# Stack loads spread over 44 steps, the second matrix block loaded apart, and a unit's steps moved, in a kernel of attention and Fourier mixing

## The chip, the cores and the metric

The kernel runs on one core of a Trainium2 chip. The metric is the device time of one execution in microseconds; three runs of the kernel before stand behind its median. One further execution was taken by the hardware profiler, and all rows of a trace come from it. The engines are called PE (matmul), PEld (its weight loads), DVE (vector), ACT (scalar), POOL (GpSimd) and SP (sync, which here only issues DMAs). Each works through its own instructions in order and waits for the others by semaphores. DMAs are issued by SP and by POOL.

## The reference

The input is one sequence of 2048 rows with 640 columns. Two results are computed from it, 32-head attention with heads of 20 columns and the real part of a two-dimensional Fourier transform, and a sigmoid gate of each row mixes them.

```python
def reference(A_x, A_wqkv, A_wo, B_x, B_dft_seq_re, B_dft_seq_im, B_dft_hid_re, B_dft_hid_im, gate_w):
    # _A_ref: attention, 32 heads of 20
        scores = jnp.einsum("bhqd,bhkd->bhqk", q, k) * (Dh ** -0.5)
        p = _softmax(scores, axis=-1)
        o = jnp.einsum("bhqk,bhkd->bhqd", p, v)
    # _B_ref: transform along the columns, then along the rows, real part
        a = jnp.einsum("bsd,ed->bse", x, dft_hid_re)
        b = jnp.einsum("bsd,ed->bse", x, dft_hid_im)
        y = jnp.einsum("ts,bse->bte", dft_seq_re, a) - jnp.einsum("ts,bse->bte", dft_seq_im, b)
    ...
    x = A_x
    g = _sigmoid((x * gate_w).sum(-1, keepdims=True))
    return g * a + (1 - g) * b
```

## The kernel before, in words

**Units and steps.** The main loop walks through 32 units. A unit is a pair of heads and half of the queries (1024 of them); two units make a pair of heads. A unit has 32 steps, so there are 1024 steps; a step scores 128 keys against 512 queries for both heads. Scores are computed twice. The first time (L159) gives the maxima: VectorE reduces each block of 512 (L161). The second time (L682) takes two more rows, in which the maximum is subtracted inside the matmul, and ACT takes the exponential (L684). The maxima run 41 steps ahead of the exponentials. Every four steps make a cycle whose order of scores (`e`, `m`) and fill work (`F`) is written out in `ORDER`; at its end (`B`) the averages over the values follow (L445).

**The fill work** that stands between the scores is the Fourier half: first the transform along the columns (L298), then, from step 228, the one along the rows (L520), 16 DFT steps to a tile of output, with a saving of products in which matrices and halves are first added (`PRODUCTS`). One matrix block of 128 x 1024 serves eight DFT steps. `load_c` loads it in one or two parts of 512 KB on SP's queue (L410); its `finish` adds the two parts on POOL (L416) and splits the sum into a leading and a trailing part (L102, L103), which the matmuls read as `part`. A block is loaded at DFT step 0 of eight, three blocks ahead, and finished at DFT step 4, two blocks ahead. The first part goes to a tile `raw` of three buffers, the second to `raw2` of two. In the same way `load_a` loads the other operand (L425) and POOL prepares it (L430, L102, L103). At the end of a tile POOL adds the result to what stands in memory (L551).

**Stacks.** `load_stack` brings the keys (`kst`) and queries (`qst`) of the next pair from memory in twelve DMAs on POOL's queue (L632): four for the keys, four for the queries of the pair's first unit, four for those of its second. They are emitted at steps 2, 4, ... 24 of the pair that runs. The maxima of the next pair begin in that pair's step 23, those of its second unit in step 55. Pair 9, say, is loaded in units 15 and 16, counted as the units whose results leave then.

**The end of a unit.** `unit_end` copies the averages to `o` and hands seven pieces of work to later steps (L485): the row sums go to memory (L459) and come back in another shape (L462), DVE takes their reciprocal (L465), this goes to memory (L468) and comes back spread over partitions as `rb` (L472), POOL multiplies (L475), and `o` is stored (L483). All of these DMAs are on SP's queue.

**The rows of the maxima.** When a unit's maxima are done, `max_chain` transposes them and splits them on DVE, and two steps later SP writes four rows into `qst` (L198, L199). This happens in step 26 of a unit, and the exponentials of the unit that needs them begin in step 32, that is, with the next unit.

**The order** within an engine is the order of emission. `at_step` puts work off to the beginning of a later step, in the order in which it was handed over.

Of the kernel before, what the change touches and what calls it, by code (L numbers as in the profile page):

```python
# [10 lines left out]
F32 = mybir.dt.float32  # L11
# [7 lines left out]
P = 128  # L19
# [10 lines left out]
NU = 2 * NP  # L30
# [15 lines left out]
PRODUCTS = (  # L46
# [7 lines left out]
)  # L54
HT = NS // 2
UNITS = len(PRODUCTS) * HT


def f32(ap):
    return ap.bitcast(F32)  # L60
# [3 lines left out]
def mix_kernel(ctx: ExitStack, tc: tile.TileContext, xa, wqk, wb, cdft, wo, out):  # L64
    nc = tc.nc
    pe, act, dve, pool, sp = nc.tensor, nc.scalar, nc.vector, nc.gpsimd, nc.sync
# [48 lines left out]
    def pair_tile():  # L115
        return work.tile([P, 2, 512], F32, name="p", bufs=5)

    def raw_tile():
        return work.tile([P, 1024], F32, name="raw", bufs=3)

    def part_tile():
        return work.tile([P, 2, 1024], R, name="part", bufs=3)
# [4 lines left out]
    def load_stack(p):  # L127
        kt, qt = kst[p % 2], qst[p % 2]
        u = S // 2
        for t, o, two, one, cs in ((kt, D, 0, 2, slice(0, S)), (qt, 0, 1, 0, slice(0, u)), (qt, 0, 1, 0, slice(u, S))):  # L130
            for h in range(2):
                r = (2 * p + h) * DH
                b = 64 * h
                rows = slice(o + r, o + r + DH)
                yield f32(t[b + two * DH : b + (two + 2) * DH, cs]), qk_scr[:, rows, cs]
                yield f32(t[b + one * DH : b + (one + 1) * DH, cs]), qk_scr[0, rows, cs]
# [8 lines left out]
    def at_step(i, fn):  # L145
        later.setdefault(i, []).append(fn)
# [254 lines left out]
    cfin, rest = [], []  # L401

    def load_c(g):
        n, j = divmod(g, 2)
        n, t = divmod(n, HT)
        raws = []
        for i, (_, th, ri) in enumerate(PRODUCTS[n][0]):
            raw = apool[0].tile([P, 1024], F32, name="raw2", bufs=2) if i and apool else raw_tile()
            o = (2 * ri + j) * 1024
            sp.dma_start(raw, cdft[th * HT + t, :, o : o + 1024])  # L410
            raws.append(raw)

        def finish():
            c = cparts[g] = part_tile()
            if len(raws) > 1:
                pool.tensor_tensor(raws[0], raws[0], raws[1], op=ALU.add if PRODUCTS[n][0][1][0] > 0 else ALU.subtract)  # L416
            split(c[:, 0], c[:, 1], raws[0], pool, pool)

        return finish

    def load_a(n, s):
        raws = []
# [27 lines left out]
    def unit_end(i, n):  # L450
        o = pa.tile([P, 512], F32, name="o")
        act.activation(o, av, AF.Copy)
        lc = pa.tile([P, 16], F32, name="lc")
        rb = pa.tile([P, 512], F32, name="rb")

        q = pool if n == NU - 1 else sp

        def store_l():
            q.dma_start(l_scr[n], o.rearrange("(j r) c -> j r c", j=4)[:, DH])  # L459

        def load_l():
            q.dma_start(lc, l_scr[n].rearrange("j (a b) -> (j a) b", b=16))  # L462

        def recip():
            dve.reciprocal(lc, lc)  # L465

        def store_r():
            q.dma_start(r_scr[n].rearrange("j (a b) -> (j a) b", b=16), lc)  # L468

        def load_r():  # L470
            for j in range(4):
                q.dma_start(rb[32 * j : 32 * j + 32, :], r_scr[n, j : j + 1].to_broadcast([32, 512]))  # L472

        def norm():
            pool.tensor_tensor(o, o, rb, op=ALU.mult)  # L475

        def store_o():
            for qc in range(2):
                for h in range(2):
                    j = 2 * qc + h  # L480
                    t0 = (n % 2) * (S // 2) + qc * 512
                    r = (2 * (n // 2) + h) * DH
                    q.dma_start(o_scr[r : r + DH, t0 : t0 + 512], o[32 * j : 32 * j + DH, :])  # L483

        steps = (1, 4, 10, 12, 15, 23, 25) if n < NU - 2 else (1, 4, 10, 12, 15, 19, 21)  # L485
        for k, fn in zip(steps, (store_l, load_l, recip, store_r, load_r, norm, store_o)):
            if n == NU - 1:
                rest.append(fn)
            else:
                at_step(i + k, fn)  # L490
# [7 lines left out]
    def dft_step(g):  # L498
        n, t, s = g // NS // HT, g // NS % HT, g % NS
        if s == 0:  # L500
            new_y(0), new_y(1)
            outs[n, t] = []
            for _, th, hf in PRODUCTS[n][2]:
                tt = th * HT + t
                y = None
                if (tt, hf) in signs:
                    y = apool[0].tile([P, HE], F32, name="yt", bufs=4)
                    sp.dma_start(y, y_scr[tt, :, hf * HE : (hf + 1) * HE])
                outs[n, t].append(y)
        if s % 8 == 0 and g // 8 + 3 < 2 * UNITS:  # L510
            cfin.append(load_c(g // 8 + 3))
        if s % 8 == 4 and cfin and g // 8 + 2 < 2 * UNITS:
            cfin.pop(0)()
        c = cparts[g // 8]
        cs = slice((s % 8) * P, (s % 8 + 1) * P)
        a = at[n % 2, s]
        for z, (cz, az) in enumerate(((0, 0), (0, 1), (1, 0))):
            for h in range(2):
                r = slice(64 * h, 64 * h + 64)
                pe.matmul(yp[h][:, :HE], c[r, cz, cs], a[r, az], start=s == 0 and z == 0, stop=s == NS - 1 and z == 2)  # L520
            if z < 2:
                yield
        w = g % (HT * NS) - 16
        if n + 1 == len(PRODUCTS) and w >= 0:
            d, r = divmod(w, 8)
            if r == 0 and d < ND:
                wos[d] = raw_tile()[:, :D]
                sp.dma_start(wos[d], wo[:, d])
            if r == 5 and d < ND:
                raw = wos.pop(d)  # L530
                for h in range(2):
                    wos[d, h] = a_tile(1, 2 * d + h)
                    split(wos[d, h][:, 0], wos[d, h][:, 1], raw[:, h * HE : (h + 1) * HE], pool, pool)
        if s == NS - 1:
            m = apool[0].tile([P, HE], F32, name="m", bufs=2)
            y0, y1 = yp[0][:, :HE], yp[1][:, :HE]

            def read():
                act.activation(m, y0, AF.Copy)
                dve.tensor_tensor(m, y1, m, op=ALU.add)  # L540

            extras.append((now[0], read))
            for out_, y in zip(PRODUCTS[n][2], outs.pop((n, t))):
                extras.append((now[0] + 5, functools.partial(finish_y, out_, t, m, y)))
        yield
# [29 lines left out]
    apool = []  # L575
# [25 lines left out]
    HID = 4 * NS - HEAD  # L601
# [26 lines left out]
    def begin(i):  # L628
        now[0] = i
        n, s = divmod(i, 32)  # L630
        for fn in later.pop(i, ()):
            fn()  # L632
        if s % 2 == 0:
            flush()
        if s == 0 and n % 2 == 0:
            p = n // 2
            if p + 1 < NP:
                at_step(i + 6, functools.partial(load_v, p + 1))
                for j, args in enumerate(load_stack(p + 1)):
                    at_step(i + 2 + 2 * j, functools.partial(pool.dma_start, *args))  # L640
        if i < total:
            pts[n, s // 2, s % 2] = pair_tile()

    def end(i):
        if start + 2 <= i < start + 2 + HT:
            for k in range(2):
                at_step(i + 3, load_a(0, 2 * (i - start - 2) + k))
        if i % 4 == 2:
            c = i // 4
            if c + HEAD in (NS, 2 * NS):  # L650
                at_step(i + 2, load_wb(3 + (c + HEAD) // NS, pool, pool))
            if c in (HID - 5, HID - 3):
                at_step(i + 4, load_c((c - HID + 5) // 2))
            if c == HID + 1:
                cfin.append(load_c(2))
        if total - 10 <= i < total - 4 and i % 2 == 0:
            tt = (i - total + 10) // 2
            fins[tt] = load_o(tt)
        if i == total - 3:
            fins[0]()  # L660
# [71 lines left out]
    for tt in range(NS):  # L732
        y, o = ys.pop(tt), ops.pop(tt)
# [53 lines left out]
```

## Time and profile before

| | us |
|---|---|
| median of 3 runs | 1962.29 |
| lowest, highest | 1959.55, 1966.06 |
| the profiled execution | 1970.17 |
| its span, first to last instruction | 1968.4 |
| first start of the exponentials' scores, last | 270.8, 1889.2 |
| maxima on DVE (L161, 2048 of 683 ns) | 1287.9 |
| exponentials on ACT (L684, 2048 of 599 ns) | 1081.3 |
| POOL: sums and splits of matrix blocks (L416, L102, L103) | 187.8, 116.2, 267.0 |

A group's row gives the line, the engine, the operation, what it writes and reads, the count, then busy time and the mean of one in nanoseconds, then the engine's idle time just before these instructions and what ended it. A row of a timeline gives start and duration in microseconds, and in brackets the idle time before it and its releaser. The mean granted clock of TensorE was 0.990 of full speed over the span.

### The profile page before, as it was taken

To read this page: it belongs to the slowest core of one execution; us is meant where nothing else is said; L and a number is where in the kernel's file an instruction comes from. 1 tells how busy PE (TensorE), PEld (TensorE's weight loads), DVE (VectorE), ACT (ScalarE), POOL (GpSimd) and SP (SyncE) were. 2 spreads that over 40 slices of the span, in tenths; PEclk is the share of its full clock that TensorE was granted. 3 is DMA by queue.
4 is the path that set the end of the run, shared out by engine and by line. 5 is a ranking of instruction groups with operands and counts; after the bars stand their busy time and mean duration, and the time that the engine had idled before them with its cause. 6 is when DMAs were issued, how large, how long until landed. Compare 5 with 4: busy or idle time off the path is not lost. (4 is left out here: it accounts for less than half of the span.)

```text
span 1968.4 us, 43695 instructions
## 1 busy us (share of the span) xinstructions
PE 1932.7 (98%) x17080; PEld 1384.1 (70%) x17080; DVE 1455.3 (74%) x2419; ACT 1212.9 (62%) x2337; POOL 1045.3 (53%) x975
## 2 busy tenths in 40 slices
PE   8999999999999999999999999999999999999999
PEld 7987767777775666666666666666666666666679
DVE  4145568888897888887888878788888887888323
ACT  4221147777776676776676766666777766766741
POOL 1210001111005989556569967995786789687522
PEclk9999999999998999999999999999999999999999
DMA  7663321313124485435366746654554565554355
GB/s 222 172 170 126 131 97 46 81 57 81 38 62 144 160 227 149 122 114 142 99 174 198 195 152 183 211 170 121 145 176 124 179 171 173 158 153 148 97 158 183
DMA packets 196414, 281.02 MB, mean 143 GB/s; under 512 B 73272, under 2 KB 137816, under 8 KB 194288
## 3 DMA queue, kind: packets, MB, share of 16 engines
q1 hardware_dynamic: 158992, 246.20, 40.7%
q0 software_dynamic: 37216, 32.03, 6.7%
q8 instruction: 134, 2.20, 0.5%
q14 instruction: 72, 0.59, 0.1%
HBM read 213.81 MB, written 63.70 MB: 141 GB/s over the span
## 5 line engine op out<-in xcount | busy, mean ns | idle before, releaser
L161 DVE TENSOR_REDUCE mx<-ps 128x1 f32<-128x512 f32 x2048 | 1287.9, 683 | 203.6 <-PE ps L159 176.6
L684 ACT ACTIVATE p<-ps 128x512 f32<-128x512 f32 x2048 | 1081.3, 599 | 457.4 <-PE ps L159 254.3
L159 PE MATMUL ps<-kst,qst 60*128 60x512 f32 x2048 | 777.8, 427 | 9.8 <-DVE mx L161 3.8
L682 PE MATMUL ps<-qst,kst 62*128 62x512 f32 x2048 | 705.3, 424 | 7.8 <-DMA qst<-m 6.2
L520 PE MATMUL yp<-a,part 64*128 64x320 f32 x5376 | 687.5, 309 | 0.1
L520 PEld LDWEIGHTS yp<-a,part 64*128 64x128 f32 x5376 | 594.3, 186 | 15.5 <-DVE m L540 0.3
L445 PE MATMUL av<-p,v 128*21 128x512 f32 x4096 | 500.1, 605 | 0.1
L682 PEld LDWEIGHTS ps<-qst,kst 62*128 62x128 f32 x2048 | 339.0, 185 | 220.4 <-DVE mx L161 179.3
L159 PEld LDWEIGHTS ps<-kst,qst 60*128 60x128 f32 x2048 | 365.5, 185 | 39.5 <-DVE mx L161 12.5
L103 POOL TENSOR_TENSOR part<-raw,part 128x1024 fp32r<-128x1024 f32 x112 | 267.0, 2384 | 9.0
L445 PEld LDWEIGHTS av<-p,v 128*21 128x21 f32 x4096 | 98.8, 101 | 228.8 <-issue 225.2
L298 PE MATMUL yp<-wb,xs 64*128 64x320 f32 x1920 | 239.8, 312 | 3.1 <-ACT raw L306 3.0
L298 PEld LDWEIGHTS yp<-wb,xs 64*128 64x128 f32 x1920 | 209.7, 189 | 8.3 <-ACT raw L306 3.6
L416 POOL TENSOR_TENSOR raw<-raw,raw 128x1024 f32<-128x1024 f32 x78 | 187.8, 2407 | 17.5 <-DMA raw<-in_cdft 13.1
L102 POOL CAST part<-raw 128x1024 fp32r<-128x1024 f32 x112 | 116.2, 1037 | 124.6 <-PE yp L520 81.8
L102 POOL CAST wb<-raw 128x966 fp32r<-128x966 f32 (+1 forms) x4 | 3.4, 852 | 216.8 <-DMA raw<-in_wb 196.8
L551 POOL TENSOR_TENSOR yt<-yt,m 128x320 f32<-128x320 f32 x64 | 55.3, 873 | 114.2 <-DVE m L540 110.7
L475 POOL TENSOR_TENSOR o<-o,rb 128x512 f32<-128x512 f32 x32 | 41.3, 1292 | 130.9 <-DMA rb<-r_scr 71.1
L103 POOL TENSOR_TENSOR a<-araw,a 128x320 fp32r<-128x320 f32 x112 | 97.5, 871 | 9.0
L103 DVE TENSOR_TENSOR p<-ps,p 128x512 fp32r<-128x512 f32 x40 | 27.5, 691 | 94.8 <-ACT p L100 92.1
L106 PE MATMUL ps<-xs,part 128*128 128x512 f32 x200 | 80.6, 403 | 7.4 <-ACT xs L100 6.1
L100 ACT ACTIVATE p<-ps 128x512 fp32r<-128x512 f32 x40 | 23.8, 597 | 102.6 <-PE ps L108 102.6
(67 smaller groups left out, 1337.4 us busy)
## 6 DMA issues: line engine op xcount, KB each, us to landing
raw<-in_cdft SPq DMA_DIRECT2D x192, 512.0 KB
araw<-a_scr SPq DMA_DIRECT2D x192, 160.0 KB
qk_scr<-p SPq DMA_DIRECT2D x40, 512.0 KB
kst<-qk_scr POOLq DMA_DIRECT2D x32, 320.0 KB, 12.5
qst<-qk_scr POOLq DMA_DIRECT2D x64, 160.0 KB, 8.5
a_scr<-raw SPq DMA_DIRECT2D x64, 160.0 KB
yt<-y_scr SPq DMA_DIRECT2D x64, 160.0 KB
y_scr<-yt SPq DMA_DIRECT2D x64, 160.0 KB
```

The costliest lines, as they stand in the source:

```text
L102: e1.tensor_copy(dst1, src)
L103: e2.tensor_tensor(dst2, src, f32(dst1), op=ALU.subtract)
L106: pe.matmul(ps, st1, mv1, start=first, stop=False)
L159: pe.matmul(ps, q[b : b + KROWS, qt * P : (qt + 1) * P], k[b : b + KROWS, kc * 512 : (kc + 1) * 512], start=True, stop=True)
L161: return lambda: dve.tensor_reduce(mx[n][:, h, qt, kc : kc + 1], ps, axis=AX.X, op=ALU.max)
L298: pe.matmul(yp[h][:, :HE], xs[r, xz, d, cs], w[r, wz, d, :HE], start=d == 0 and z == 0, stop=d == ND - 1 and z == 2)
L416: pool.tensor_tensor(raws[0], raws[0], raws[1], op=ALU.add if PRODUCTS[n][0][1][0] > 0 else ALU.subtract)
L445: pe.matmul(av[32 * j : 32 * j + DH + 1, :], v[:, kt, h * (DH + 1) : (h + 1) * (DH + 1)], pp[qc][:, h, :], start=kt == 0, stop=kt == NS - 1)
L520: pe.matmul(yp[h][:, :HE], c[r, cz, cs], a[r, az], start=s == 0 and z == 0, stop=s == NS - 1 and z == 2)
L551: pool.tensor_tensor(y, y, m, op=ALU.add if sg == signs[tt, hf] else ALU.subtract)
L682: pe.matmul(pt, k[b : b + KROWS + 2, kt * P : (kt + 1) * P], q[b : b + KROWS + 2, qc * 512 : (qc + 1) * 512], start=True, stop=True)
L684: act.activation(pts[n, kt, qc][:, h], pt, AF.Exp, scale=float(DH) ** -0.5)
```

## The change

Three places are touched.

1. `load_c` returns two functions, `load` and `finish`. Each call of `load` issues one part. The first part is issued at DFT step 0 of eight as before, the second at DFT step 4, directly after the `finish` of the block before it. The first blocks, before the loop of DFT steps runs, still get both parts at once.
2. For all units but the last two, the steps of `unit_end` are 1, 5, 13, 15, 18, 24, 26 in place of 1, 4, 10, 12, 15, 23, 25.
3. The twelve stack DMAs are emitted at steps 2, 4, 6, 8, 11, 13, 15, 17, 32, 36, 40, 44 in place of 2 to 24. The last four are the queries of the second unit. Their order among themselves is the same.

```diff
-        for i, (_, th, ri) in enumerate(PRODUCTS[n][0]):
-            raw = apool[0].tile([P, 1024], F32, name="raw2", bufs=2) if i and apool else raw_tile()
-            o = (2 * ri + j) * 1024
-            sp.dma_start(raw, cdft[th * HT + t, :, o : o + 1024])
-            raws.append(raw)
+
+        def load():
+            i = len(raws)
+            if i < len(PRODUCTS[n][0]):
+                _, th, ri = PRODUCTS[n][0][i]
+                raws.append(apool[0].tile([P, 1024], F32, name="raw2", bufs=2) if i and apool else raw_tile())
+                o = (2 * ri + j) * 1024
+                sp.dma_start(raws[i], cdft[th * HT + t, :, o : o + 1024])
...
-        return finish
+        load()
+        return load, finish
...
-        steps = (1, 4, 10, 12, 15, 23, 25) if n < NU - 2 else (1, 4, 10, 12, 15, 19, 21)
+        steps = (1, 5, 13, 15, 18, 24, 26) if n < NU - 2 else (1, 4, 10, 12, 15, 19, 21)
...
-        if s % 8 == 4 and cfin and g // 8 + 2 < 2 * UNITS:
-            cfin.pop(0)()
+        if s % 8 == 4:
+            if cfin and g // 8 + 2 < 2 * UNITS:
+                cfin.pop(0)[1]()
+            if cfin:
+                cfin[0][0]()
...
-                for j, args in enumerate(load_stack(p + 1)):
-                    at_step(i + 2 + 2 * j, functools.partial(pool.dma_start, *args))
+                for j, args in zip((2, 4, 6, 8, 11, 13, 15, 17, 32, 36, 40, 44), load_stack(p + 1)):
+                    at_step(i + j, functools.partial(pool.dma_start, *args))
...
-                at_step(i + 4, load_c((c - HID + 5) // 2))
+                load, finish = load_c((c - HID + 5) // 2)
+                load()
+                at_step(i + 4, finish)
             if c == HID + 1:
                 cfin.append(load_c(2))
+                cfin[0][0]()
```

## The prediction

> **What bounds the kernel now.** First the page: span, engine times and the PE groups with their idle time.
>
> ```profile
> span 1968.4 us, 43695 instructions
> PE 1932.7 (98%) x17080; PEld 1384.1 (70%) x17080; DVE 1455.3 (74%) x2419; ACT 1212.9 (62%) x2337; POOL 1045.3 (53%) x975
> L159 PE MATMUL ps<-kst,qst 60*128 60x512 f32 x2048 | 777.8, 427 | 9.8 <-DVE mx L161 3.8
> L682 PE MATMUL ps<-qst,kst 62*128 62x512 f32 x2048 | 705.3, 424 | 7.8 <-DMA qst<-m 6.2
> ```
>
> PE is busy 98% of the span, and the change takes no matmul away. So it can only win or lose where PE stands still, and in the slow clock that follows. PE's own timeline has four such places in the main loop that lie beside moved work:
>
> ```profile
> 905.83 0.50 PE L159 MATMUL ps<-kst,qst 60*128 60x512 f32 x1 [2.12 <-DVE mx L161]
> 1142.68 0.83 PE L682 MATMUL ps<-qst,kst 62*128 62x512 f32 x2 [3.02 <-DMA qst<-m]
> 1247.37 0.59 PE L682 MATMUL ps<-qst,kst 62*128 62x512 f32 x2 [3.22 <-DMA qst<-m]
> 1638.32 0.76 PE L159 MATMUL ps<-kst,qst 60*128 60x512 f32 x1 [3.30 <-DMA qst<-qk_scr]
> ```
>
> What each costs is read from ten-microsecond windows: us, busy time of PE, PEld, DVE, ACT, POOL, then the granted clock and the DMA engines' share.
>
> ```profile
> 609.00:619.00 10.00, 7.01 (x47) 4.99 (x47) 4.08 (x8) 3.81 (x7) 7.37 (x6) 0.74 0.17 60
> 903.00:913.00 10.00, 7.88 (x62) 4.26 (x61) 5.78 (x11) 4.30 (x10) 7.44 (x9) 0.83 0.70 191
> 1139.00:1149.00 10.00, 6.97 (x49) 3.34 (x49) 4.07 (x7) 3.66 (x8) 9.35 (x6) 0.83 0.19 70
> 1244.00:1254.00 10.00, 6.78 (x49) 3.75 (x48) 4.63 (x9) 4.12 (x9) 9.65 (x10) 0.83 0.33 99
> 1634.00:1644.00 10.00, 6.70 (x41) 3.44 (x38) 4.00 (x8) 3.00 (x6) 9.70 (x9) 0.69 0.68 205
> 1010.00:1020.00 10.00, 10.00 (x100) 7.05 (x88) 7.63 (x14) 6.84 (x14) 5.37 (x6) 1.00 0.88 224
> ```
>
> The last row is an undisturbed stretch. A window's loss is its idle time plus (1 - clock) x 10 us: 2.1 + 1.7 = 3.8 us at 905; 3.0 + 1.7 = 4.7 at 1142; 3.2 + 1.7 = 4.9 at 1247; 3.3 + 3.1 = 6.4 at 1638. Together 19.8 us, the most that the change can win there. The window at 609 (a loss of 5.6 us) belongs to the change of stage, where the edits move little; it stays.
>
> A step is (1889.2 - 270.8) / 1024 = 1.58 us, from the first and last start here:
>
> ```profile
> L682 PE MATMUL ps<-qst,kst x2048: 386/397/792, 270.8 to 1889.2; 62*128 62x512 f32 x187
> ```
>
> The stalls lie at steps about 399 (unit 11's results, pair 7's load), 543 (unit 15, pair 9), 607 (unit 17, pair 10) and 855 (unit 25, pair 14): always a unit in which a stack is loaded.
>
> **The reciprocal.** At 905 PE waited for VectorE's maxima, and VectorE for this:
>
> ```profile
> 904.98 0.25 DVE L465 RECIPROCAL lc<-lc 128x16 f32<-128x16 f32 x1 [2.22 <-DMA lc<-l_scr]
> ```
> ```profile
> 892.81 0.32 SPq L462 DMA_DIRECT2D lc<-l_scr  x1
> ```
>
> The small load took 904.98 - 892.81 = 12.2 us. The change issues it one step later and the reciprocal three steps later: two steps (3.2 us) more distance against 2.22 us of waiting. Behind the reciprocal on VectorE stand the maxima, whose banks PE waits for, so the whole stall goes: **-3.8 us**. Bounds: -3.8, and 0 if the load, now behind one more issue of L425 on SP, lands over 3 us later than it did.
>
> **The normalization, and the rows behind it.** At 1142 and 1247 PE waited for the rows of the maxima (L198, L199). SP issues them behind the stores of `o` (L483), and those wait for POOL's L475:
>
> ```profile
> 1131.83 1.30 POOL L475 TENSOR_TENSOR o<-o,rb 128x512 f32<-128x512 f32 x1
> ...
> 1236.51 1.30 POOL L475 TENSOR_TENSOR o<-o,rb 128x512 f32<-128x512 f32 x1
> ```
> ```profile
> 1237.83 1.42 SPq L483 DMA_DIRECT2D o_scr<-o  x4
> 1239.30 1.72 SPq L410 DMA_DIRECT2D raw<-in_cdft  x2
> 1241.11 0.68 SPq L198 DMA_DIRECT2D qst<-m  x1
> ```
>
> L475 starts with no gap: POOL is behind its queue, and what counts is how much stands ahead. These are POOL's prices:
>
> ```profile
> L632 POOL DMA_DIRECT2D qst<-qk_scr x120 | 69.3, 585 | 25.2 <-DMA kst<-qk_scr 25.1
> L430 POOL TENSOR_TENSOR araw<-araw 128x320 f32<-128x320 f32 x80 | 69.9, 874 | 5.9 <-DMA araw<-a_scr 5.5
> L102 POOL CAST a<-araw 128x320 fp32r<-128x320 f32 x112 | 50.4, 450 | 21.4 <-DMA araw<-a_scr 16.2
> L103 POOL TENSOR_TENSOR a<-araw,a 128x320 fp32r<-128x320 f32 x112 | 97.5, 871 | 9.0
> L551 POOL TENSOR_TENSOR yt<-yt,m 128x320 f32<-128x320 f32 x64 | 55.3, 873 | 114.2 <-DVE m L540 110.7
> ```
>
> In these units three of the four issues for the second unit's queries (steps 18, 20, 22) stood ahead of L475 and now stand 14 steps or more behind it: 3 x 0.585 = 1.76 us earlier. L475 itself goes from step 23 to 24; nothing else in POOL's program changes place with it in units 15 and 17. (In units 9, 13 and 28 part or all of a matrix block's work slips ahead; none of them is among the late ones.) SP keeps its order: stores of `o`, now at step 26, then the rows of the same step. Further, one of the two L410 issues between L483 and the rows goes away, about half of the 1.72 us at 1239; I count 0.5 us at 1142 and 1.1 us at 1247. At 1142 the idle time falls from 3.0 to 3.0 - 1.76 - 0.5 = 0.8 us. Does a stall this short still lose the clock? The nearest rows:
>
> ```profile
> 262.93 0.50 PE L106 MATMUL ps<-xs,part 128*128 128x512 f32 x1 [1.31 <-ACT part L100]
> ```
> ```profile
> 260.00:270.00 10.00, 8.56 (x37) 6.40 (x36) 2.14 (x3) 1.82 (x3) 0.00 (x0) 1.00 0.34 130
> ```
>
> 1.31 us idle kept clock 1.00, 2.12 us at 905 lost it. So 0.8 is left of 4.7: **-3.9 us**. At 1247 the second matrix block takes back a part (next); its rows come about 1.76 + 1.1 - 0.8 = 2.1 us sooner, 1.1 us idle is left and with some chance of the clock I take 1.5: **-3.4 us**. Bounds for both: 0 (POOL finds another wait and is no sooner) and -9.6.
>
> [...]
>
> **The second matrix block** is loaded four DFT steps later in the program, but SP runs ahead of its emission, so often it moves by a few issues only. Around pair 10's load:
>
> ```profile
> 1201.43 0.86 SPq L410 DMA_DIRECT2D raw<-in_cdft  x2
> 1202.34 0.42 SPq L437 DMA_DIRECT2D v<-v_scr  x1
> 1207.61 0.85 SPq L425 DMA_DIRECT2D araw<-a_scr  x2
> ```
> ```profile
> 1215.43 2.43 POOL L416 TENSOR_TENSOR raw<-raw,raw 128x1024 f32<-128x1024 f32 x1 [4.26 <-PE av L445]
> ```
>
> In the changed order it comes directly behind the load of `v`: about 0.9 us later. POOL's wait before the sum at 1215 cannot be for PE's averages, which L416 does not read; I take it for the block's landing, and the price as **0.8 us** on POOL (used above). From 0.4 (an issue) to 4.3 (the wait doubles). Elsewhere POOL runs ahead of its need and a wait there is covered by its later waits (L551's 114.2 us above).
>
> **The first unit's queries** keep their place in POOL's program but for the last piece, which goes from step 16 to 17 and so behind one preparation of `a`: 0.874 + 0.450 + 0.871 = 2.2 us, in pair 9 also behind one L551 (3.1 us). Their landing and PE's first use:
>
> ```profile
> L632 POOL DMA_DIRECT2D qst<-qk_scr x1: 542/542/542, 1118.1 to 1118.1; - x1
> ...
> DMA to landing us min/median/max: 6.1/6.1/6.1
> ```
> ```profile
> L632 POOL DMA_DIRECT2D qst<-qk_scr x2: 519/576/634, 1221.4 to 1222.0; - x2
> ...
> DMA to landing us min/median/max: 7.7/7.9/8.2
> ```
> ```profile
> 1125.87 0.40 PE L159 MATMUL ps<-kst,qst 60*128 60x512 f32 x1
> ```
> ```profile
> 1230.32 0.40 PE L159 MATMUL ps<-kst,qst 60*128 60x512 f32 x1
> ```
>
> Pair 9 lands at 1124.2 with 1.7 us to spare, pair 10 at 1229.7 with 0.6 us, pair 14 is already late (1638). At full price: 3.1 - 1.7 = 1.4, 2.2 - 0.6 = 1.6, and 2.2 us more: 5.2 us. Transfers that leave these units may shorten the landing; I take half, **+2.6 us**. Bounds: -6.4 (the stall at 1638 goes) and 5.2 + 3 x 1.7 of clock = +10.3.
>
> **Other moves, at nothing.** `rb` has 6 steps from its issue to L475 in place of 8. Where POOL runs early it will wait there, and L475 still comes before step 24; if that cover went, POOL would lose up to two steps, 3.2 us, in such a unit. SP's wait for `r_scr` before L472 keeps its three steps, with the loads of `a` and of the matrix blocks queued behind it as now, only later in the unit. The second unit's queries, first needed at step 55, are issued by step 44: 11 steps, 17 us, for landings of 6 to 8 us in the rows above. POOL in those units carries the same four issues, 2.3 us, ahead of a later L475. Without this cover each pair would stall as at 1638, up to 6.4 us.
>
> **Sum.** -3.8 - 3.9 - 3.4 + 2.6 = -8.5 us. The profiled execution took 1970.17 us (span 1968.4); the median of the runs is 1962.29, and I carry the sum over unchanged: **1953.8, forecast 1954 us**, -0.43%.
>
> **Rivals.** *Slower: the last query piece decides.* If every one of the three is late at full price and loses the clock (+10.3), and POOL, waiting for matrix blocks that come late, brings L475 no sooner, then only the reciprocal is won: -3.8 + 10.3 = +6.5, 1968.8 us. It decides from 0.6 us of lateness in pair 10. For it: that margin, and DMA engines at 0.68 around 1638; against it: idle under 1.3 us kept the clock. 0.18. *Nothing to speak of: the wait is only handed on.* The reciprocal is won, L475 gains nothing, the pieces cost their 2.6: -1.2, 1961.1 us. For it: POOL's 4.26 us gap ahead of L475 at 1215, into which earlier work falls. 0.34. *All four stalls go*, the unloaded units' DMA relief reaching pair 14: -19.8, 1942.5 us. Against it: the piece at 1638 is issued later, not sooner. 0.10. *The change does not do what it says*: the second block is not apart in time, since SP runs ahead; true in the rows above, and without a time of its own.
>
> **How the numbers follow.** 0.38 for the forecast, 0.10, 0.34 and 0.18 for the others. A change under 0.3% (5.9 us) cannot be told from none here. Faster: 0.38 + 0.10 = 0.48; within: 0.34; slower: 0.18. The likeliest one's own range is 1951 (the query pieces cost nothing) to 1958 (one of the rows' terms is not won); the cases on both sides widen it to 1943 (all four stalls) and 1967 (most of the slower case).
>
> **What would show it.** Right: no gap before the reciprocal at step 397; L475 in units 15 and 17 some 1 to 2 us sooner by step and the rows' stalls under 1 us at full clock. The query term: PE waiting for `qst<-qk_scr` at steps 535, 599, 855. Wrong, if these gaps are gone and the time is not, if new waits for `part` or `raw` stand before PE, or if the stalls simply sit in other units.

## The result, and the profile after

The changed kernel is slower by 0.5%. Ratios are taken over runs on the same chips.

| | us |
|---|---|
| before, median of 6 runs beside it | 1960.68 (1958.47 to 1966.06) |
| changed, median of 6 runs | 1973.48 (1971.20 to 1974.39) |
| ratio | 1.0053, 95% interval 1.0039 to 1.0067 |
| profiled execution, before and changed | 1970.17, 1974.10 |
| forecast | 1954, range 1943 to 1967 |

The two profiled executions lie closer together than the medians: that of before, at 1970.17, is longer than each of its six runs. First the groups of PE and POOL in the changed kernel (L692 was L682, L419 was L416, L479 was L475, L639 was L632):

```profile
L159 PE MATMUL ps<-kst,qst 60*128 60x512 f32 x2048 | 778.3, 428 | 24.1 <-DMA qst<-qk_scr 15.0 <-issue 4.9 <-DVE mx L161 1.7
L692 PE MATMUL ps<-qst,kst 62*128 62x512 f32 x2048 | 703.5, 423 | 1.5 <-DVE mx L161 1.1 <-ACT p L694 0.3
...
L419 POOL TENSOR_TENSOR raw<-raw,raw 128x1024 f32<-128x1024 f32 x78 | 187.0, 2397 | 65.5 <-DMA raw<-in_cdft 52.5 <-PE ps L159 6.9 <-PE ps L692 5.5
...
L479 POOL TENSOR_TENSOR o<-o,rb 128x512 f32<-128x512 f32 x32 | 41.4, 1292 | 165.2 <-DMA rb<-r_scr 158.1 <-DMA out_y<-p 4.0 <-DMA yt<-y_scr 2.4
```

The wait for the rows of the maxima (6.2 us ahead of L682 before) is gone. The wait for the queries ahead of L159 has grown from 3.3 us to 15.0, and the 4.9 us put down to "issue" stands at the same kind of place, below. POOL's idle time ahead of the sums of matrix blocks has grown to 65.5 us. This is the group that answers to it in the kernel before:

```profile
L416 POOL TENSOR_TENSOR raw<-raw,raw 128x1024 f32<-128x1024 f32 x78 | 187.8, 2407 | 17.5 <-DMA raw<-in_cdft 13.1 <-PE av L445 4.3
```

PE's timeline of the changed kernel has four stalls of more than 2.2 us in the main loop, all before the first maxima of a new pair (pairs 5, 9, 10 and 14):

```profile
723.37 0.76 PE L159 MATMUL ps<-kst,qst 60*128 60x512 f32 x1 [4.58 <-DMA qst<-qk_scr]
...
1128.37 0.76 PE L159 MATMUL ps<-kst,qst 60*128 60x512 f32 x1 [4.85 <-issue]
...
1235.68 0.76 PE L159 MATMUL ps<-kst,qst 60*128 60x512 f32 x1 [5.33 <-DMA qst<-qk_scr]
...
1642.41 0.76 PE L159 MATMUL ps<-kst,qst 60*128 60x512 f32 x1 [5.12 <-DMA qst<-qk_scr]
```

The ten-microsecond windows around them, and two at the places of before's stalls behind the reciprocal and the rows:

```profile
719.00:729.00 10.00, 5.63 (x39) 3.34 (x41) 3.40 (x9) 1.96 (x5) 9.71 (x9) 0.83 0.62 192
1124.00:1134.00 10.00, 5.63 (x35) 3.22 (x35) 3.10 (x5) 1.82 (x4) 9.65 (x9) 0.66 0.48 167
1231.00:1241.00 10.00, 5.32 (x30) 2.67 (x30) 2.48 (x4) 1.32 (x3) 9.71 (x9) 0.70 0.76 217
1637.00:1647.00 10.00, 4.88 (x30) 2.70 (x31) 3.26 (x6) 2.26 (x5) 9.71 (x8) 0.71 0.67 211
903.00:913.00 10.00, 10.00 (x104) 7.87 (x100) 9.32 (x16) 7.66 (x15) 5.75 (x6) 1.00 0.57 162
1139.00:1149.00 10.00, 10.00 (x96) 6.71 (x90) 7.77 (x14) 7.18 (x15) 9.76 (x8) 1.00 0.39 110
```

By the prediction's own count (idle time and lost clock) the four lose 6.1, 7.8, 7.7 and 8.0 us, 29.6 together, against 6.4 us for late queries before. Where the reciprocal and the rows of unit 15 had cost 3.8 and 4.7 us, nothing is lost any more.

Why the queries are late is read at pair 10, from three views: SP's timeline before and after, then POOL's after. In the kernel before, SP issued both parts of the block that POOL sums at 1195.36 together:

```profile
1189.16 0.95 SPq L410 DMA_DIRECT2D raw<-in_cdft  x2
1197.33 0.55 SPq L459 DMA_DIRECT2D l_scr<-o  x1
```

After, the second part stands behind the store of the row sums (L463, before L459), and that waits until the unit ends:

```profile
1189.11 0.43 SPq L414 DMA_DIRECT2D raw<-in_cdft  x1
1197.16 0.54 SPq L463 DMA_DIRECT2D l_scr<-o  x1
1197.81 0.39 SPq L414 DMA_DIRECT2D raw<-in_cdft  x1
```
```profile
1193.41 1.80 POOL L639 DMA_DIRECT2D kst<-qk_scr  x3 [1.66 <-PE ps L159]
1208.86 2.42 POOL L419 TENSOR_TENSOR raw<-raw,raw 128x1024 f32<-128x1024 f32 x1 [13.65 <-DMA raw<-in_cdft]
...
1214.78 0.54 POOL L639 DMA_DIRECT2D kst<-qk_scr  x1
...
1229.34 0.54 POOL L639 DMA_DIRECT2D qst<-qk_scr  x1
```

The part is issued 8 us later, when POOL has just issued the keys at 1193, and POOL's sum starts 11 us after that issue; whether the keys make the transfer longer was not tried apart. POOL stands for 13.65 us. Behind it in POOL's queue wait the last issue for the keys (1214.78, before 1204.11) and the four for the queries; the last of these comes at 1229.34 in place of 1222.0, and PE waits until 1235.7.

Ahead of the other three stalls POOL waits at a sum as well, though for less time. Here are its waits in the loads of pairs 5, 9 and 14:

```profile
702.47 2.38 POOL L419 TENSOR_TENSOR raw<-raw,raw 128x1024 f32<-128x1024 f32 x1 [5.37 <-DMA raw<-in_cdft]
...
1113.67 2.38 POOL L419 TENSOR_TENSOR raw<-raw,raw 128x1024 f32<-128x1024 f32 x1 [3.92 <-DMA raw<-in_cdft]
...
1614.09 2.38 POOL L419 TENSOR_TENSOR raw<-raw,raw 128x1024 f32<-128x1024 f32 x1 [5.47 <-PE ps L692]
```

The last row's releaser cannot be what the sum waited for, since L419 reads no scores; it is taken for the block's landing too.

### The profile page after: what moved, and what is told of

It reads as the page before. It is cut to its first block, busy times and chain, and to the rows that moved or that the text cites. A ratio compares the mean times of both kernels' runs of the same rounds, so it can differ in the third digit from the quotient of the medians.

```text
span 1972.3 us, 43657 instructions
## 1 busy us (share of the span) xinstructions
PE 1928.4 (98%) x17080; PEld 1382.7 (70%) x17080; DVE 1458.0 (74%) x2419; ACT 1212.6 (61%) x2337; POOL 1045.9 (53%) x975
## 5 line engine op out<-in xcount | busy, mean ns | idle before, releaser
L159 PE MATMUL ps<-kst,qst 60*128 60x512 f32 x2048 | 778.3, 428 | 24.1 <-DMA qst<-qk_scr 15.0
L692 PE MATMUL ps<-qst,kst 62*128 62x512 f32 x2048 | 703.5, 423 | 1.5 <-DVE mx L161 1.1
L527 PEld LDWEIGHTS yp<-a,part 64*128 64x128 f32 x5376 | 596.3, 187 | 15.4 <-DVE m L547 0.3
L692 PEld LDWEIGHTS ps<-qst,kst 62*128 62x128 f32 x2048 | 337.1, 185 | 212.1 <-DVE mx L161 167.5
L159 PEld LDWEIGHTS ps<-kst,qst 60*128 60x128 f32 x2048 | 365.9, 185 | 53.1 <-issue 24.6
L419 POOL TENSOR_TENSOR raw<-raw,raw 128x1024 f32<-128x1024 f32 x78 | 187.0, 2397 | 65.5 <-DMA raw<-in_cdft 52.5
L479 POOL TENSOR_TENSOR o<-o,rb 128x512 f32<-128x512 f32 x32 | 41.4, 1292 | 165.2 <-DMA rb<-r_scr 158.1
```

The costliest lines, as they stand in the source:

```text
L159: pe.matmul(ps, q[b : b + KROWS, qt * P : (qt + 1) * P], k[b : b + KROWS, kc * 512 : (kc + 1) * 512], start=True, stop=True)
L692: pe.matmul(pt, k[b : b + KROWS + 2, kt * P : (kt + 1) * P], q[b : b + KROWS + 2, qc * 512 : (qc + 1) * 512], start=True, stop=True)
```

## The experiments

Three theories were put on record. A: POOL waits at the sum for the late second part, and the stack's issues queued behind it come late. B: the last query piece's place at step 17 is enough by itself. C: the unit's steps cost it, with POOL waiting for `rb`. Every kernel was timed in five rounds against the kernel before.

| run | median, us | ratio, 95% interval | POOL idle ahead of the sums, us |
|---|---|---|---|
| both parts at once | 1952.68 | 0.9952, 0.9936 to 0.9967 | 19.4 |
| parts apart alone | 1977.23 | 1.0082, 1.0065 to 1.0099 | 63.6 |
| unit steps alone | 1952.99 | 0.9959, 0.9945 to 0.9974 | 15.4 |
| stack alone | 1958.07 | 0.9984, 0.9974 to 0.9995 | 17.6 |
| apart, pieces at 10 to 16 | 1960.53 | 1.0003, 0.9990 to 1.0017 | 58.5 |
| together, pieces at 10 to 16 | 1949.48 | 0.9946, 0.9930 to 0.9962 | 14.9 |
| apart, second part earlier | 1951.52 | 0.9961, 0.9947 to 0.9974 | 6.4 |
| together, pieces at 9 to 12 | 1944.08 | 0.9927, 0.9909 to 0.9945 | 19.5 |
| apart, pieces at 9 to 12 | 1956.77 | 0.9978, 0.9966 to 0.9990 | 64.3 |
| second part at DFT step 2 | 1963.63 | 1.0002, 0.9988 to 1.0017 | 41.6 |

The median of before beside these lay at 1960.6 to 1962.0 us.

**Both parts at once**, the rest of the change kept (`load()` issues one part).

```diff
         load()
+        load()
         return load, finish
```

> The changed kernel, but both parts of a matrix block are issued at DFT step 0, as before; the stack's and the unit's steps stay changed. Theory A (POOL waits at the sum for the late second part, and the stack issues behind it come late): POOL's idle time ahead of the sums falls from 65.5 us to about 17, the four stalls at the queries go or shrink to under 2 us, and the time is 1950 to 1958 us. Theory B (the last query piece's place at step 17, behind a preparation of a, is enough by itself): stalls of 3 us or more stay in pairs 9, 10 and 14, time 1966 to 1972. Theory C (the unit's steps, with POOL waiting for rb): the time stays at 1970 to 1974.

It took 1952.68 us: with that one undone the change is a gain. Theory C falls: POOL still waits 164.4 us for `rb` ahead of the normalization, as in the changed kernel (158.1), and the loss is gone. POOL's group of sums in this kernel:

```profile
L419 POOL TENSOR_TENSOR raw<-raw,raw 128x1024 f32<-128x1024 f32 x78 | 186.9, 2396 | 19.4 <-DMA raw<-in_cdft 10.5 <-PE ps L693 5.0 <-DMA araw<-a_scr 3.7
```

Two stalls at the queries are left, of 2.9 us in pair 9 and 3.6 in pair 14, so the expected "under 2 us" was too low:

```profile
1121.90 0.47 PE L159 MATMUL ps<-kst,qst 60*128 60x512 f32 x1 [2.88 <-issue]
...
1625.64 0.76 PE L159 MATMUL ps<-kst,qst 60*128 60x512 f32 x1 [3.63 <-DMA qst<-qk_scr]
```

**Parts apart alone**: the changed kernel with the old unit steps and the old stack steps.

```diff
-        steps = (1, 5, 13, 15, 18, 24, 26) if n < NU - 2 else (1, 4, 10, 12, 15, 19, 21)
+        steps = (1, 4, 10, 12, 15, 23, 25) if n < NU - 2 else (1, 4, 10, 12, 15, 19, 21)
...
-                for j, args in zip((2, 4, 6, 8, 11, 13, 15, 17, 32, 36, 40, 44), load_stack(p + 1)):
-                    at_step(i + j, functools.partial(pool.dma_start, *args))
+                for j, args in enumerate(load_stack(p + 1)):
+                    at_step(i + 2 + 2 * j, functools.partial(pool.dma_start, *args))
```

> The kernel before with the second part of a block issued at DFT step 4 alone. Theory A: slower than before by as much as the whole change or more, since the rows' stalls of units 15 and 17 stay or grow on top of late queries: 1970 to 1985 us, POOL idle ahead of the sums 50 to 70 us. Theory B: the last query piece keeps step 16, so no more than 3 us of new stalls: 1960 to 1965. Theory C: 1958 to 1963.

1977.23 us, as theory A had it. Its PE groups show both kinds of stall side by side, late queries and late rows:

```profile
L159 PE MATMUL ps<-kst,qst 60*128 60x512 f32 x2048 | 778.1, 428 | 19.3 <-DMA qst<-qk_scr 9.6 <-DVE mx L161 7.1 <-ACT p L694 0.6
L692 PE MATMUL ps<-qst,kst 62*128 62x512 f32 x2048 | 704.3, 423 | 5.4 <-DMA qst<-m 3.9 <-DVE mx L161 1.1 <-ACT p L694 0.3
```

**Unit steps alone**: the kernel before with `steps = (1, 5, 13, 15, 18, 24, 26)`.

> The kernel before with the unit's steps 1, 5, 13, 15, 18, 24, 26 alone. Theories A and B: the stall behind the reciprocal goes, 3.8 us; the normalization one step later with all eleven issues ahead of it may cost the rows up to 1.6 us in units 15 and 17: 1956 to 1962 us. Theory C: 1966 us or more, POOL's idle time ahead of the normalization up by 30 us as in the changed kernel, and PE stalls with it.

1952.99 us, better than the expected 1956 to 1962. This part alone wins as much as the change with both parts at once (1952.68). The rows, which were expected to lose up to 1.6 us, gained: PE waits 1.6 us for `qst<-m` in its trace, in place of 6.2. Why is read below, under the rows.

**Stack alone**: the kernel before with the twelve issues at the changed steps.

> The kernel before with the stack's issues at 2, 4, 6, 8, 11, 13, 15, 17, 32, 36, 40, 44 alone. Theory A: the normalization comes 1.8 us sooner in units 15 and 17 and the rows' stalls shrink; the last query piece is 2 to 3 us later in pairs 9, 10 and 14: 1953 to 1962 us. Theory B: stalls of 3 us or more at the queries in pairs 9, 10 and 14: 1966 to 1972. Theory C: 1955 to 1962.

1958.07 us, a small gain, as A and C expected and B did not.

**Apart, pieces at 10 to 16**: the changed kernel with only the first unit's queries put back.

```diff
-                for j, args in zip((2, 4, 6, 8, 11, 13, 15, 17, 32, 36, 40, 44), load_stack(p + 1)):
+                for j, args in zip((2, 4, 6, 8, 10, 12, 14, 16, 32, 36, 40, 44), load_stack(p + 1)):
```

> The changed kernel with the first unit's queries at steps 10, 12, 14, 16 again; the parts stay apart. Theory A (POOL's wait at the sum decides): POOL's idle time ahead of the sums stays at 50 to 66 us, at least three of the four stalls at the queries stay, each 1 to 3 us shorter: 1964 to 1972 us. Theory B (the last piece's place at step 17 decides): the stalls fall under 2 us, 1953 to 1960 us.

1960.53 us, between the two expectations, so A in its plain form missed. POOL still waits 58.5 us, but the one step that the pieces are earlier is worth 13.0 us of medians (1973.48 to 1960.53).

**Together, pieces at 10 to 16**: the same with both parts at once.

> Both parts at DFT step 0, and the first unit's queries at steps 10, 12, 14, 16; the unit's steps and the second unit's queries stay changed. Against the run with both parts at once, this shows what the place of the last piece costs by itself. If it costs what POOL's prices say (2.2 to 3.1 us in pairs 9 and 14, with some clock), 1946 to 1951 us; if it costs nothing, 1952 to 1954 us.

1949.48 us: here the same step of the pieces is worth 3.2 us (1952.68 to 1949.48), and this difference is not clear of the scatter, as the two ratios' intervals overlap. The two costs are not a sum. Either alone costs 3.2 (late pieces) or 11.0 us (late part, 1949.48 to 1960.53), both together 24.0 (1949.48 to 1973.48).

**Apart, but the second part earlier**: it is issued four DFT steps before the first part, into a third buffer.

```diff
...
+            if g // 8 + 4 < 2 * UNITS:
+                early.append(load_c(g // 8 + 4))
+                early[0][0](1)
...
```

> The changed kernel, but the second part is issued four DFT steps before the first one, not four after it, with a third buffer for it. Theory A in its narrow form (what hurts is that the second part comes late): POOL's idle time ahead of the sums at 10 to 25 us and 1946 to 1956 us. Its rival (what hurts is that the two parts are apart, each behind other loads in SP's queue): 1964 us or more.

1951.52 us, and POOL's wait ahead of the sums is the shortest of all, 6.4 us, below the expected 10 to 25. So it is not being apart that costs here, but coming late. The third buffer was not tried by itself.

**Together, pieces at 9 to 12.**

```diff
-                for j, args in zip((2, 4, 6, 8, 11, 13, 15, 17, 32, 36, 40, 44), load_stack(p + 1)):
+                for j, args in zip((2, 4, 6, 8, 9, 10, 11, 12, 32, 36, 40, 44), load_stack(p + 1)):
```

> Both parts at DFT step 0, and the first unit's queries at steps 9, 10, 11, 12. If the last stalls are those of late query pieces, they go in pairs 9 and 14: 1944 to 1950 us. If the queries then only crowd with the keys and land no sooner, 1951 to 1955 us.

1944.08 us, faster than both kernels. Its PE groups have no wait for `qst` among the first three releasers any more:

```profile
L159 PE MATMUL ps<-kst,qst 60*128 60x512 f32 x2048 | 773.8, 425 | 4.3 <-DVE mx L161 1.7 <-ACT p L695 0.6 <-DVE p L103 0.5
L693 PE MATMUL ps<-qst,kst 62*128 62x512 f32 x2048 | 704.2, 423 | 1.9 <-DVE mx L161 1.4 <-ACT p L695 0.3
```

**Apart, pieces at 9 to 12**: the same pieces in the changed kernel.

> The changed kernel (parts apart) with the first unit's queries at steps 9, 10, 11, 12. If POOL's wait for the late part hurts only through the query pieces behind it, the earlier pieces take most of it away although POOL waits as long (50 to 66 us ahead of the sums): 1944 to 1952 us. If the wait hurts by another way too (rows, part, maxima on DVE), it stays over 1956 us.

1956.77 us: the wait hurts by another way too. The queries are in time, and the rows are late instead, since the normalization stands behind the same sums in POOL's queue. PE's group, its timeline, and the window around the largest of three such stalls:

```profile
L692 PE MATMUL ps<-qst,kst 62*128 62x512 f32 x2048 | 704.0, 423 | 8.5 <-DMA qst<-m 6.9 <-DVE mx L161 1.1 <-ACT p L694 0.3
```
```profile
1133.03 0.62 PE L692 MATMUL ps<-qst,kst 62*128 62x512 f32 x2 [3.00 <-DMA qst<-m]
```
```profile
1130.00:1140.00 10.00, 7.00 (x52) 4.24 (x52) 4.34 (x8) 4.18 (x8) 9.79 (x7) 0.83 0.50 142
```

**Second part at DFT step 2** in place of 4.

```diff
-        if s % 8 == 4:
...
+        if s % 8 == 2 and cfin and g // 8 + 3 < 2 * UNITS:
+            cfin[-1][0]()
+        if s % 8 == 4 and cfin and g // 8 + 2 < 2 * UNITS:
+            cfin.pop(0)[1]()
```

> The changed kernel with the second part at DFT step 2 in place of 4. Theory A: POOL's idle time ahead of the sums between 17 and 65 us, about 30 to 45, and the time between 1952.7 (both at step 0) and 1973.5 (at step 4): 1957 to 1969 us. If only the place behind the finish of the block before it matters, it is as with both at once: 1951 to 1955.

1963.63 us and 41.6 us of POOL's waiting: both lie between those with both parts at once and those of the changed kernel, so the cost grew with the lateness here.

## Why the prediction was wrong

**The reciprocal: right.** VectorE does not wait for it any more (the changed kernel's row is below), and the window at 903 has PE at 10.00 and clock 1.00. The -3.8 us were won. With the old steps the stall stays: 2.02 us in the trace of parts apart alone.

```profile
908.76 0.24 DVE L469 RECIPROCAL lc<-lc 128x16 f32<-128x16 f32 x1
```

**The normalization and the rows: the stalls went, but not in the forecast way.** No wait for `qst<-m` is left at L692; the prediction had kept 0.8 and 1.5 us. But the normalization itself, which was to come 1 to 2 us sooner, came at nearly the same time in unit 15 (1131.83 before) and 3.1 us later in unit 17 (1236.51 before):

```profile
1131.39 1.28 POOL L479 TENSOR_TENSOR o<-o,rb 128x512 f32<-128x512 f32 x1
...
1239.65 1.27 POOL L479 TENSOR_TENSOR o<-o,rb 128x512 f32<-128x512 f32 x1
```

Two other things made the rows come in time. PE had just stood 4.85 and 5.33 us at the queries of the same load, so it asked for the rows later; that is luck as far as the forecast goes. And SP got from the stores of `o` to the last of the rows faster. Here it is before, then after:

```profile
1133.16 1.41 SPq L483 DMA_DIRECT2D o_scr<-o  x4
1134.61 0.64 SPq L508 DMA_DIRECT2D yt<-y_scr  x1
1135.30 0.90 SPq L410 DMA_DIRECT2D raw<-in_cdft  x2
...
1139.70 0.63 SPq L199 DMA_DIRECT2D qst<-m  x1
```
```profile
1132.69 1.41 SPq L487 DMA_DIRECT2D o_scr<-o  x4
1134.48 0.68 SPq L198 DMA_DIRECT2D qst<-m  x1
...
1136.63 0.64 SPq L199 DMA_DIRECT2D qst<-m  x1
```

With the stores at step 26 nothing stands between them and the rows. SP took 6.5 us from the first store to the last row before and 3.9 after, at pair 10 6.5 and 4.0; the prediction gave this 0.5 and 1.1 us. It belongs to the unit's steps: in their run alone SP takes 3.8 us here. So the prediction had the gains in the wrong place. It gave the unit's steps the reciprocal's 3.8 us and the stack's steps the rest, 7.3 - 2.6 = 4.7; alone they won 7.7 and 2.6 us of medians. The stack's moves do bring the normalization sooner where POOL does not wait: together with pieces at 9 to 12 it comes 4.1 and 0.9 us after VectorE's first maxima of pairs 9 and 10, with no stall ahead, in place of 5.4 and 5.6 before. Apart with the same pieces it comes 9.4 and 7.8 us after them, and the rows are late.

**The second matrix block: the step that failed.** It was priced at 0.8 us, at most 4.3, from one place around 1202, where SP ran ahead and the part was to move by a few issues. At the block just ahead of that one, SP's next instruction was the store of the row sums, which waits for the end of the unit: SP stood there from 1189.54 to 1197.16, 7.6 us, and the part was moved to the far side of that wait. POOL's wait there was 13.65 us, and 65.5 in place of 17.5 over the whole run. Around 1202 itself the reading did not hold either. The second part was to go out right behind the load of `v`, about 0.9 us later; it went out at 1208.78, after 7.2 us in which SP waited, by the profile, for a landing of `raw`:

```profile
1201.08 0.43 SPq L441 DMA_DIRECT2D v<-v_scr  x1
1208.78 0.33 SPq L414 DMA_DIRECT2D raw<-in_cdft  x1
```

The sentence that elsewhere a wait "is covered by its later waits" was an error too: in the four loads with a stall, no wait of POOL over 0.3 us stands between the sum that waits and the last issue of the first unit's queries, so nothing covers it.

**The query pieces: the term that was mis-sized by it.** Predicted +2.6 us with a bound of +10.3; measured 29.6 - 6.4 = +23.2 us in the windows. The 2.2 us behind the preparation of `a` were there, but they were set against margins of 0.6 and 1.7 us taken from the kernel before, in which POOL did not wait as long. With parts together the pieces' place cost 3.2 us of medians, near the 2.6, within the scatter said above.

**The sum.** Without the second block's part, the forecast of -8.5 us stands beside 1952.68 - 1960.71 = -8.0 us. That is partly luck, since two terms were off in opposite directions: in that trace no stall at the rows is left (-9.6 in place of -7.3), and the queries cost 4.6 us in pair 9 and 6.5 in pair 14, +4.7 against before in place of +2.6. In the profiled executions of before and changed the terms are +23.2 - 3.8 - 4.7 - 4.9 = +9.8, and the change of stage, which was to stay, got shorter. Its windows, before and then after:

```profile
590.00:650.00 60.00, 56.24 (x413) 33.50 (x409) 43.90 (x73) 36.42 (x70) 36.14 (x46) 0.89 0.54 165
```
```profile
590.00:650.00 60.00, 56.43 (x452) 33.42 (x446) 46.56 (x78) 38.97 (x76) 35.52 (x44) 0.97 0.52 166
```

The clock alone makes (0.97 - 0.89) x 60 = 4.8 us less there, so about +5.0 us are left of the sum, and the spans differ by 1972.3 - 1968.4 = +3.9. What changed this stage was not tried apart. The medians differ by 12.8 us: the traced execution of before was 9.5 us longer than its median, and where a usual one is shorter no trace shows.

**The rivals.** The slower rival had the right place, late query pieces, and the right helper, late blocks that keep the normalization from coming sooner, but had them at 1968.8 us and a chance of 0.18. It let them cancel the rows' gain; they did not, for the two reasons above, until the pieces were moved out of the way (the run apart with pieces at 9 to 12).

## What to carry to other kernels

A load that was put off on SP's queue moved here to the far side of the next wait on that queue, 8 us later, not by the steps written in the program: look for the next blocking instruction at every place where it occurs, not at one. The same held for a gain: a store moved by one step freed the rows behind it from the loads in between, and the last row came 3.9 us after the first store in place of 6.5. POOL, which waited 13.65 us for the load, handed the wait on to the DMA issues of the next stack queued behind it: the last piece for pair 10's first unit came at 1229.34 in place of 1222.0. Two delays in one queue in front of one deadline did not add up: 3.2 and 11.0 us alone were 24.0 together. This fits a margin that each of them uses up for the other, which is argued and not measured.

## What the runs showed of the hardware

Stalls of PE of about 2 us cost clock in some places and none in others, and length alone did not decide it. 1.31 us kept the clock at 1.00 in the prediction's row and 2.12 us lost it; the unit steps alone show one of 1.60 us that lost it, and the changed kernel one of 2.17 us that kept it. PE's timeline and the window in the kernel with the unit steps alone:

```profile
1135.65 0.59 PE L682 MATMUL ps<-qst,kst 62*128 62x512 f32 x2 [1.60 <-DMA qst<-m]
```
```profile
1131.00:1141.00 10.00, 8.40 (x66) 4.75 (x63) 5.44 (x10) 5.11 (x11) 9.78 (x7) 0.83 0.19 64
```

The same two views in the changed kernel, with the window behind it, in which the clock is 1.00 as well:

```profile
614.45 0.93 PE L298 MATMUL yp<-wb,xs 64*128 64x320 f32 x2 [2.17 <-ACT raw L306]
```
```profile
609.00:619.00 10.00, 7.71 (x73) 5.37 (x69) 6.48 (x12) 5.17 (x10) 7.05 (x4) 1.00 0.20 69
619.00:629.00 10.00, 9.72 (x58) 3.86 (x56) 8.50 (x16) 6.59 (x14) 0.56 (x2) 1.00 0.31 88
```

So the first cost about twice its idle time, 1.6 us idle and 0.17 x 10 = 1.7 us of clock, and the second its idle time alone. The prediction's two nearest rows, 1.31 us kept and 2.12 us lost, are thus no bounds of a length at which the clock is lost; for a stall of this size both prices belong in the range.
